# Attention and feed-forward on one core: the first batch's q and k in token halves from two queues, and a planner that models the DMA queues as rings

## The chip, the cores and the metric

The kernel runs on one core of a Trainium2 chip. The metric is device time in microseconds (us) of one execution, as the median of several runs. A profile shows one execution; its span runs from the first to the last instruction of the core. TensorE (PE) multiplies matrices, ScalarE (ACT) does activations and issues some DMAs, VectorE (DVE) and GpSimd (POOL) do elementwise work, SyncE (SP) only issues DMAs.

## The reference

There are 8 batches of 8 heads, 576 tokens, head size 64. Attention has a forget gate per token; its output, tokens by 512, goes through a gated feed-forward network (512 to 1536 and back).

```python
scores = scale * np.matmul(q, k.transpose(0, 1, 3, 2))
cum = np.cumsum(np.log(np.clip(f, 0.0001, 1.0)), axis=-1)
scores = np.where(causal, -1e9, scores + cum[..., :, None] - cum[..., None, :])
attn = softmax(scores)                       # max-shifted, over the last axis
x = (attn @ v)                               # (B, H, S, D) -> (B*S, H*D)
xn = x / np.sqrt(np.mean(x * x, -1, keepdims=True) + 1e-6) * rms_g
g = xn @ w_gate
out = (g * sigmoid(g) * (xn @ w_val)) @ w_out
```

## The kernel before

The work is written as some thousands of pieces (`plan.add`): name, engine, an assumed duration, what it depends on, which buffers it takes and gives back, a priority. `Plan.run` is a list scheduler at build time: it plays the pieces through with their assumed durations, and the order in which they start there is the order in which the instructions are emitted. On the chip each engine then works its own list strictly in that order, and waits for real. So a plan's durations never run on the chip; only its order does.

On PE the pieces are of kind A (attention: transposes, scores, values) or F (feed-forward: gates and projections). `LEAD` and `UNTIL` steer the mix: A comes first as long as less of A is done than a line that reaches all of A when the share `UNTIL` of F is done.

```python
behind = a_done < self.lead + (a_total - self.lead) * min(1.0, f_done / (f_total * self.until))
first = "A" if behind else "F"
```

A batch b goes through these steps. q and k come from memory into `st` tiles and are cast to bf16 `ld` tiles. For b = 0 and 1 (`PE_TURN`) PE transposes them (L462) and ACT and DVE keep the results in `QK` (L467); for the others SP issues DMA transposes (L493, the last 64 tokens L496). Scores (L561) go to PSUM, ACT exponentiates (L569), POOL masks the diagonal blocks (L577), PE multiplies with the scaled V (values, L596), DVE normalizes into `x` (L606). Then ACT squares the five token blocks (L613), POOL makes the root (L622), DVE scales to `xn` (L626), and `xn` is transposed into `xT`, by PE for b = 0 and 1 (L651), else by DMA (L645). Batch 0 is split: part one (`HEAD`) does tokens 0 to 255, part two (`REST`) the others.

The feed-forward goes by groups of tokens: g0 and g1 have 256, g2 to g9 have 512. A group has 12 steps of gate and value matmuls (L747, four each), ACT tanh `th` (L752), DVE `ga` and `hT` (L756, L762); then the projections (L768, 12 matmuls for 128 tokens), ACT's copy to `ores` (L773) and the store, which ACT issues (L776). Group g(n) from g2 on needs the `xT` of batch n-1, g1 that of batch 0.

q and k of batch 0 come as four units, each of two heads (`load_runs`: 128 partitions, 512 tokens, 256 KB), k and q in turn, all issued by SP. DVE casts k, POOL casts q. The weights are loaded by POOL in eight pieces of columns; in the plan all of them wait for q's last cast.

The framework gives every DMA that SP or ACT issues one of eight semaphores in turn, in the order in which they are emitted. Before it issues, the engine waits until the DMA that had this semaphore before, eight places ahead, has landed. In the built program's order this wait reads `DMAHW0_49` to `DMAHW7_49`. The planner has a pool of eight for it (`hw`), of which it takes whichever is free.

The planner before keeps one clock for all DMAs: each transfer begins when the last one has ended.

Of the kernel before, what the change touches and what calls it, by code (L numbers as in the profile page):

```python
# [11 lines left out]
ACT = mybir.ActivationFunctionType  # L12
# [9 lines left out]
LEAD, UNTIL = 30.0, 0.74  # L22
Q_AHEAD, V_AHEAD, T_AHEAD = 1.6, 0.9, 0.95
SPLIT, PE_TURN = (0,), (0, 1)
GROUPS = ((0, 256), (256, 512)) + tuple((a, a + 512) for a in range(512, B * S, 512))
N_ST, N_LD, N_PT, N_XN = 10, 6, 4, 5
SV_PRIO = -0.7
# [25 lines left out]
class Plan:  # L53
# [7 lines left out]
    TO = {"PE": 0.20, "ACT": 0.07, "DVE": 0.07, "POOL": 0.08, "SP": 0.05}  # L61

# [11 lines left out]
    def run(self):  # L74
# [17 lines left out]
        dma_free, t, order = 0.0, 0.0, []  # L92
        n_left, next_seq = len(self.pieces), 0

# [15 lines left out]

        while n_left:
            moved = False
            for e in self.ENGINES:
# [5 lines left out]
                if e == "PE":  # L119
                    behind = a_done < self.lead + (a_total - self.lead) * min(1.0, f_done / (f_total * self.until))  # L120
                    first = "A" if behind else "F"
                    p = min(c, key=lambda p: (p.kind != first, p.prio))
                    if p.kind == "A":
                        a_done += p.dur
                    else:
                        f_done += p.dur
                else:
                    p = min(c, key=lambda p: p.prio)
                ready[e].remove(p)
# [4 lines left out]
                if p.xfer is None:  # L134
                    p.done = p.end
                else:
                    dma_free = max(dma_free, p.start + 0.7) + p.xfer
                    if e == "SP":
                        p.end = free_at[e] = max(p.end, dma_free - 2.0)
                    p.done = max(dma_free, p.end) + 1.7  # L140
                for pool, key in p.acq:
                    if key not in held:
# [4 lines left out]
                        slots[i] = float("inf")  # L147
                for key in p.rel:
                    left[key] -= 1
                    freed[key] = max(freed.get(key, 0.0), p.done + 0.08)  # L150
                    if not left[key]:
                        pool, i = held[key]
                        self.pools[pool][i] = freed[key]
                for u in p.users:
                    lat = 0.0 if u.eng == e and p.xfer is None else self.TO[e]
                    u.ready = max(u.ready, p.done + (0.02 if p.xfer is not None else lat))
                    u.nwait -= 1
                    if not u.nwait:
                        ready[u.eng].append(u)
# [5 lines left out]
            nxt = [f for f in free_at.values() if f > t + 1e-9]  # L165
            nxt += [p.ready for e in self.ENGINES for p in ready[e] if p.ready > t + 1e-9]
            nxt += [f for s in self.pools.values() for f in s if t + 1e-9 < f < float("inf")]
            assert nxt, "the plan is stuck at " + str([p.name for e in self.ENGINES for p in ready[e]])
            t = min(nxt)
        return sorted(order, key=lambda p: p.start)  # L170
# [28 lines left out]
def kernel(  # L199
# [65 lines left out]
    lf = plan.add("lf", "SP", 0.6, load_f, xfer=0.4, prio=(-9,), acq=[("hw", "lf"), ("pt", "pre")], rel=["lf"])  # L265
# [57 lines left out]

    def load_rg():
# [3 lines left out]
    p_rg = plan.add("rg", "SP", 0.6, load_rg, xfer=0.7, prio=(-8,), acq=[("hw", "rg")], rel=["rg"])  # L328
# [8 lines left out]
    for i, (c0, c1) in enumerate(WCH):  # L337
        for n, w, src in (("wg", wg, moe_w_gate), ("wv", wv, moe_w_val)):
            nm = f"{n}{i}"
            p = plan.add(nm, "POOL", 0.75, lambda w=w, src=src, c0=c0, c1=c1: load_w(w, src, c0, c1),  # L340
                         xfer=(22 + 37 * (c1 - c0) / 256) * 512 / 16e3, prio=(W_PRIO[i],), acq=[("sw", nm)], rel=[nm])
# [8 lines left out]
    p_wo = [plan.add(f"wo{i}", "POOL", 0.75, lambda i=i: load_wo(i), xfer=4.6, prio=(WO_PRIO[i],),  # L350
# [10 lines left out]
    def attention(b):  # L361
# [30 lines left out]
        def cast(src, dst, eng, runs=False):  # L392
# [5 lines left out]
            (nc.vector if eng == "DVE" else nc.gpsimd).tensor_copy(o, x)  # L398
# [17 lines left out]
        for u in range(4):  # L416
            for nm, src in (("k", k), ("q", q)):
                key = f"{nm}{b}.{u}"
                if not pe and nm == "k":
                    ld[nm, u] = plan.add("L" + key, "POOL", 0.9, lambda nm=nm, src=src, u=u: load_cast(nm, src, u), xfer=2.1,  # L420
                                         acq=[("ld", key), ("sw", "h" + key)], rel=["h" + key], prio=(ahead + 0.01 * u,), seq=True)
                    continue
                fn = load_runs if pe else load_rows
                a = plan.add("L" + key, "SP", 0.6, lambda fn=fn, nm=nm, src=src, u=u: fn(nm, src, u), xfer=0.78 if pe else 1.2,
                             acq=[("st", "s" + key), ("hw", "h" + key)], rel=["h" + key], prio=(ahead + 0.01 * u,), seq=True)
                eng = "DVE" if b == 0 and nm == "k" else "POOL"
                ld[nm, u] = plan.add("C" + key, eng, 0.55 if eng == "DVE" else 0.62,
                                     lambda nm=nm, u=u, eng=eng: cast((nm + "s", b, u), (nm, b, u), eng, pe), [a],
                                     acq=[("ld", key)], rel=["s" + key], prio=(ahead + 0.01 * u,))
        key = f"qk{b}"  # L430
        a = [plan.add(f"L{key}{t}", "SP", 0.45, lambda t=t, src=src: load_tail(t, src), xfer=0.6,
# [406 lines left out]
```

## Time and profile before

| | us |
|---|---|
| runs | 430.77, 428.05, 429.48; median 429.48 |
| profiled execution | 429.98 |
| its span | 428.2 |
| outside the span | 1.8 |
| PE busy in the span | 375.9 (88%) |

A row in order of time reads: start, duration, engine, line, operation, output and input tile, count; in brackets the idle time of the engine just before, and what ended it. SPq and ACTq are the queues on which SP and ACT issue DMAs. PEclk is the granted TensorE clock, 1.00 being 2.4 GHz and 0.50 being 1.2 GHz.

### The profile page before, as it was taken

Reading aid. Unit: us, or ns where it says so; the run is one execution under the profiler, and the core shown is the slowest. Engines: PE = TensorE matmul, PEld = TensorE weight load, DVE = VectorE, ACT = ScalarE, POOL = GpSimd, SP = SyncE. Lnnn points to the kernel's source line nnn. Section 1 sums busy time; section 2 is a strip of 40 time slices with the busy share of each in tenths; the row PEclk is TensorE's granted clock in tenths of the full one; section 3 lists DMA queues with packets and bytes.
Section 4 is the critical chain, followed back from the end, with each engine's and each line's share of the span. In section 5 each row is a group of like instructions: output and inputs, shape, how many; then the busy total and the mean of one; then the engine's idle time right before and its main releaser. Section 6 shows DMA issues by size and latency. Waiting matters only on the chain.

```text
span 428.2 us, 8052 instructions
## 1 busy us (share of the span) xinstructions
PE 375.9 (88%) x3085; PEld 195.0 (46%) x3085; DVE 239.6 (56%) x462; ACT 218.7 (51%) x361; POOL 163.2 (38%) x259
## 2 busy tenths in 40 slices
PE   1559889969998799799997999499989996999996
PEld 1327657634643355335543554145534552444442
DVE  5654846745763577347623686057546743770760
ACT  2664477557751574447655763157646752332321
POOL 3791457437530483119332843047315411000000
PEclk9999999979999899989996999889999998999999
DMA  7999995769927997369967983799457004001002
GB/s 232 194 282 196 205 185 57 100 147 167 88 51 143 215 102 91 105 145 174 101 124 147 181 87 81 135 221 74 77 148 143 2 26 119 10 2 73 24 2 99
DMA packets 155847, 50.89 MB, mean 119 GB/s; under 512 B 141280, under 2 KB 151008, under 8 KB 155808
## 3 DMA queue, kind: packets, MB, share of 16 engines
q1 hardware_dynamic: 119872, 33.06, 43.3%
q0 software_dynamic: 30752, 7.87, 18.7%
q10 hardware_dynamic: 5184, 9.44, 6.2%
q8 instruction: 24, 0.39, 0.4%
q14 instruction: 15, 0.12, 0.1%
HBM read 38.16 MB, written 9.44 MB: 111 GB/s over the span
## 4 chain that ended last, share of the span: by engine, by line
PE 61%; DVE 11%; DMA 7%; ACT 7%; issue 5%; POOL 5%; SPq 3%; ACTq 1%; POOLq 0%; DVEq 0%
PE ff L747 41%; PE ff L768 10%; PE sc L561 5%; DVE xn L626 3%; DMA xT<-xn 3%; DVE x L606 3%; ACT junk L613 3%; PE po L596 2%; DVE ga L756 2%; DMA QK<-ld 2%; SPq L645 2%; PE ff L596 2%; POOL PT L577 2%; DVE hT L762 1%; ACT th L752 1%
## 5 line engine op out<-in xcount | busy, mean ns | idle before, releaser
L747 PE MATMUL ff<-xT,wg 128*128 128x512 bf16 (+1 forms) x480 | 120.2, 375 | 11.5 <-DMA xT<-xn 4.5
L756 DVE SCALAR_TENSOR_TENSOR ga<-th,ff 128x512 f32<-128x512 f32 (+1 forms) x120 | 76.0, 633 | 95.5 <-ACT th L752 95.4
L747 PE MATMUL ff<-xT,wv 128*128 128x512 bf16 (+1 forms) x480 | 118.0, 370 | 6.5 <-DVE ga L756 5.7
L752 ACT ACTIVATE th<-ff 128x512 f32<-128x512 f32 (+1 forms) x120 | 66.3, 555 | 92.5 <-PE ff L747 76.0
L569 ACT ACTIVATE PT<-sc 128x1024 bf16<-128x1024 f32 (+2 forms) x100 | 95.8, 988 | 29.9 <-PE sc L561 27.8
L768 PE MATMUL ff<-wo,hT 128*128 128x512 bf16 x432 | 95.4, 379 | 0.1
L762 DVE SCALAR_TENSOR_TENSOR hT<-ga,ff 128x512 bf16<-128x512 f32 (+1 forms) x120 | 76.1, 634 | 17.9 <-PE ff L747 7.3
L747 PEld LDWEIGHTS <-wg 128*128 128x128 bf16 x480 | 45.9, 101 | 62.4 <-issue 21.3
L747 PEld LDWEIGHTS <-wv 128*128 128x128 bf16 x480 | 46.3, 101 | 57.4 <-issue 17.4
L768 PEld LDWEIGHTS <-hT 128*128 128x128 bf16 x432 | 41.9, 98 | 50.0 <-issue 0.6
L577 POOL TENSOR_SCALAR_AFFINE_SELECT PT<-PT 128x1024 bf16<-128x1024 bf16 (+1 forms) x44 | 38.4, 884 | 41.9 <-ACT PT L569 41.2
L626 DVE SCALAR_TENSOR_TENSOR xn<-x,rs,rgb 128x512 bf16<-128x512 f32 x40 | 30.6, 818 | 37.6 <-POOL rs L622 37.6
L773 ACT COPY ores<-ff 128x512 f32<-128x512 f32 x36 | 20.9, 581 | 51.6 <-PE ff L768 29.1
L561 PE MATMUL sc<-QK 64*128 64x128 bf16 (+2 forms) x328 | 31.2, 291 | 6.4 <-DMA QK<-ld 2.5
L596 PEld LDWEIGHTS <-PT 128*128 128x128 bf16 x896 | 32.6, 99 | 6.3 <-POOL PT L577 0.9
L405 POOL TENSOR_TENSOR Vs<-st,decT 128x512 bf16<-128x512 f32 x28 | 29.2, 1044 | 11.9 <-DMA st<-in_v_dram 11.8
L398 POOL CAST ld<-st 128x512 bf16<-128x512 f32 x44 | 27.8, 653 | 12.8 <-DMA st<-in_q_dram 7.8
L613 ACT ACTIVATE junk<-x 128x512 bf16<-128x512 f32 x40 | 25.2, 630 | 13.5 <-DVE x L606 10.7
L561 PEld LDWEIGHTS <-QK 64*128 64x128 bf16 x584 | 17.5, 98 | 25.4 <-issue 20.0
L521 POOL COPY K<-QT 64x256 bf16<-64x256 bf16 x16 | 7.5, 471 | 55.7 <-DMA QT<-ld 53.3
L619 POOL TENSOR_SCALAR ms<-sq 128x5 f32<-128x5 f32 (+2 forms) x9 | 1.8, 198 | 56.0 <-ACT junk L613 56.0
L377 POOL DMA_DIRECT2D ld<-in_k_dram x24 | 21.9, 916 | 0.0
(66 smaller groups left out, 224.7 us busy)
## 6 DMA issues: line engine op xcount, KB each, us to landing
out_dram<-ores ACTq DMA_DIRECT2D x36, 256.0 KB, 2.1
st<-in_q_dram SPq DMA_DIRECT2D x32, 256.0 KB, 5.2
st<-in_v_dram SPq DMA_DIRECT2D x32, 256.0 KB, 4.8
ld<-in_k_dram POOLq DMA_DIRECT2D x24, 128.0 KB, 4.2
st<-in_k_dram SPq DMA_DIRECT2D x8, 256.0 KB, 6.7
wo<-in_moe_w_out_dram POOLq DMA_DIRECT2D x2, 768.0 KB, 24.4
st<-in_q_dram SPq DMA_DIRECT2D x8, 128.0 KB, 4.9
st<-in_k_dram SPq DMA_DIRECT2D x8, 128.0 KB, 4.3
```

The costliest lines, as they stand in the source:

```text
L405: e.tensor_tensor(Vs[i][:, j, :, 0:D], t, bcast(dj, D), ALU.mult)
L561: nc.tensor.matmul(sc[:, par, c:c + n], lhsT=k_cols(r, p, kj), rhs=q_cols(r, p, q0, n), start=True, stop=True)
L569: nc.scalar.activation(T["pt", b, p][:, :, c0:c0 + n], T.pop(("sc", b, p, c0))[:, :, 0:n], ACT.Exp, scale=scale)
L577: nc.gpsimd.affine_select(out=d, in_=d, pattern=[[0, m], [1, 128]], compare_op=ALU.is_ge, fill=0.0, base=0, channel_multiplier=-1)
L596: nc.tensor.matmul(T["po", b, hs][:, qm, m, :], lhsT=w, rhs=Vs[i][:, kj, h, :], start=(kj == 0), stop=(kj == qi))
L613: nc.scalar.activation(junkp.tile([128, DM], BF16, name="junk"), T["x", b][:, j, :], ACT.Square, accum_out=T["sq", b, js][:, j:j + 1])
L626: nc.vector.scalar_tensor_tensor(xn, in0=T["x", b][:, j, :], scalar=T["rs", b, js][:, j:j + 1], in1=rgb, op0=ALU.mult, op1=ALU.mult)
L747: nc.tensor.matmul(ps[:, 0:w], lhsT=wt[:, dc, fc * 128:(fc + 1) * 128], rhs=T["xT", g][:, dc, 0:w], start=(dc == 0), stop=(dc == NDC - 1))
L752: nc.scalar.activation(t[:, 0:w], T["pg", g, fc][:, 0:w], ACT.Tanh, scale=0.5)
L756: nc.vector.scalar_tensor_tensor(a[:, 0:w], in0=T.pop(("th", g, fc))[:, 0:w], scalar=1.0, in1=T.pop(("pg", g, fc))[:, 0:w], op0=ALU.add, o ...
L762: nc.vector.scalar_tensor_tensor(T["hT", g][:, fc, 0:w], in0=T.pop(("ga", g, fc))[:, 0:w], scalar=0.5, in1=T.pop(("pv", g, fc))[:, 0:w], o ...
L768: nc.tensor.matmul(po, lhsT=T["hT", g][:, fc, j * 128:(j + 1) * 128], rhs=wo[:, fc, :], start=(fc == 0), stop=(fc == NFC - 1))
```

## The change

1. Batch 0's q and k come as other units: a unit u now holds tokens 0 to 255 (u = 0, 1) or 256 to 511 (u = 2, 3) of four heads, and is loaded by two DMAs of 64 partitions each (two heads each). q's are issued by ACT, k's by SP. `keep` writes the transposed unit to two head pairs at once. q's casts of u = 0, 1 move from POOL to ACT.
2. The order of loads in batch 0: units 0 and 1, two tiles of V, units 2 and 3, the tails, the rest of V.
3. `rms_g` is issued by ACT, not by SP.
4. In the plan each weight piece depends on another piece (`W_AFTER`): the first two on q's second cast, the others on loads of V of batch 0 and 1.
5. The planner has a ring for each issuing queue. The rings share the DMA in proportion to a weight of their first transfer, and an issue that overfills its ring of 128 holds its engine. Transfers are now (time alone, weight, descriptors in a ring).
6. `UNTIL` goes from 0.74 to 0.70. As the planner's model is another, the order of all engines is another, to the end of the program.

```diff
-LEAD, UNTIL = 30.0, 0.74
+LEAD, UNTIL = 30.0, 0.7
...
+W_AFTER = ("Cq0.1", "Cq0.1", "Lv0.2", "Lv0.2", "Lv0.40", "Lv0.40", "Lv0.40", "Lv0.40", "Lv1.3", "Lv1.3")
...
+    RING, LAND = 128, 1.75
...
+        def shares():
+            busy = [e for e in ring if ring[e]]
+            total = sum(ring[e][0][0].xfer[1] for e in busy)
+            return {e: ring[e][0][0].xfer[1] / total for e in busy}
...
+                    if c[1].eng in ("SP", "ACT") and waiting(c[1].eng) > self.RING:
+                        full[c[1].eng] = c[1]
+                        free_at[c[1].eng] = never
...
-                    dma_free = max(dma_free, p.start + 0.7) + p.xfer
-                    if e == "SP":
-                        p.end = free_at[e] = max(p.end, dma_free - 2.0)
-                    p.done = max(dma_free, p.end) + 1.7
...
-        nc.sync.dma_start(out=rgb, in_=bass.AP(tensor=moe_rms_g.tensor, offset=moe_rms_g.offset,
+        nc.scalar.dma_start(out=rgb, in_=bass.AP(tensor=moe_rms_g.tensor, offset=moe_rms_g.offset,
...
-        if b == 0:
-            for x in first_w:
-                x.deps += [ld["q", 3]]
...
+        def load_half(nm, src, u, e):
+            hh, z = divmod(u, 2)
+            t = stage((nm + "s", b, u))[e * 64:e * 64 + 64, :].rearrange("p (h c) -> p h c", h=2)
+            pp = 2 * z + e
+            (nc.scalar if nm == "q" else nc.sync).dma_start(
+                out=t, in_=src[b, 2 * pp:2 * pp + 2, hh * 256:hh * 256 + 256, :].rearrange("h (p i) d -> p h (i d)", i=4))
...
+                        eng = "DVE" if nm == "k" else "ACT" if u < 2 else "POOL"
...
+        if split:
+            load_qk((0, 1))
+            load_v((0, 1))
+            load_qk((2, 3))
+            load_tails()
+            load_v((2, 3, 4))
...
+                if split:
+                    hh, z = divmod(pp, 2)
+                    src = src.rearrange("p (i e m) -> p e m i", i=4, e=2)
+                    dst = QK[i][:, 2 * z:2 * z + 2, t, hh * 256:hh * 256 + 256].rearrange("p e (m i) -> p e m i", i=4)
...
+    for p, after in zip(first_w, W_AFTER):
+        p.deps.append(of_name[after])
```

Three places of the built programs show what moved.

**The start, ACT.** `PT_134` and `PT_136` are the forget gates (log, then exp), `rgb` is `rms_g`, `st` the loaded q. Before:

```order
L271 ACT_TABLE_LOAD
L271 ACTIVATE PT_134<-PT_134 64x576 [waits DVE_49]
L467 COPY QK0_112<-ff_172 128x512 [waits PE_49]
L285 ACT_TABLE_LOAD [waits DVE_49]
L285 ACTIVATE PT_134<-PT_134,mid_167 64x576 [waits Activation_49]
```

Now:

```order
L386 DMA rgb_107<-in_moe_rms_g_dram 128x512 [waits DMAHW0_49]
L330 ACT_TABLE_LOAD
L330 ACTIVATE PT_136<-PT_136 64x576 [waits DVE_49]
L481 DMA st_167<-in_q_dram 64x2x256 [waits DMAHW6_49]
L459 CAST ld_177<-st_124 128x512 [waits DMAHW2_49]
L459 CAST ld_180<-st_147 128x512 [waits DMAHW4_49]
L564 COPY QK0_112<-ff_182 128x2x256 [waits PE_49]
L344 ACT_TABLE_LOAD [waits DVE_49]
L344 ACTIVATE PT_136<-PT_136,mid_172 64x576 [waits Activation_49]
```

Loads and casts of q now stand in ACT's list among the gate's steps; four issues of q stand ahead of the first row shown, and three more (for u = 2 and 3) come between the exponentials of part one.

**The start, POOL.** `wg` and `wv` are the gate and value weights. Before:

```order
L398 CAST ld_162<-st_146 128x512 [waits DMAHW3_49,Pool_49]
L398 CAST ld_184<-st_151 128x512 [waits DMAHW5_49]
L398 CAST ld_203<-st_156 128x512 [waits DMAHW7_49]
L398 CAST ld_223<-st_170 128x512 [waits DMAHW1_49,DVE_49,PE_49]
L334 DMA wg_109<-in_moe_w_gate_dram 128x4x256
```

Now:

```order
L369 COPY tri_105<-tri2_142 64x64 [waits Pool_49]
L370 COPY tri_105<-tri2_142 64x64
L395 DMA wg_109<-in_moe_w_gate_dram 128x4x256
L395 DMA wv_110<-in_moe_w_val_dram 128x4x256
L680 AFFINE_SELECT PT_225<-PT_225 128x2x128 [waits Activation_49,Pool_49]
```

The casts that stood ahead of the first weight load, and waited for q, are gone from there; the first two weight loads have no wait.

**The start of group g4, DVE.** `xn` of batch 3 feeds it; `hT_2777` and, in the changed program, `hT_3064` are its output tiles, `x_2388` and `x_2275` the x of batch 3, `x_2840` that of batch 4. Before:

```order
L606 TENSOR_TENSOR x_2388<-ff_2614,rden_2645 128x5x64
L626 SCALAR_TENSOR_TENSOR xn_2719<-x_2388,rs_2698,rgb_107 128x512
L626 SCALAR_TENSOR_TENSOR xn_2722<-x_2388,rs_2698,rgb_107 128x512
L626 SCALAR_TENSOR_TENSOR xn_2740<-x_2388,rs_2698,rgb_107 128x512
L626 SCALAR_TENSOR_TENSOR xn_2743<-x_2388,rs_2698,rgb_107 128x512
L626 SCALAR_TENSOR_TENSOR xn_2746<-x_2388,rs_2698,rgb_107 128x512
L756 SCALAR_TENSOR_TENSOR ga_2774<-th_2767,ff_2756 128x512
L762 SCALAR_TENSOR_TENSOR hT_2777<-ga_2774,ff_2762 128x512
```

Now:

```order
L729 SCALAR_TENSOR_TENSOR xn_2772<-x_2275,rs_2690,rgb_107 128x512
L729 SCALAR_TENSOR_TENSOR xn_2775<-x_2275,rs_2690,rgb_107 128x512
L729 SCALAR_TENSOR_TENSOR xn_2779<-x_2275,rs_2690,rgb_107 128x512
L708 RECIPROCAL rden_2841<-po_2803 128x5
L709 TENSOR_TENSOR x_2840<-po_2803,rden_2841 128x5x64
L708 RECIPROCAL rden_2857<-ff_2823 128x5
L709 TENSOR_TENSOR x_2840<-ff_2823,rden_2857 128x5x64
L708 RECIPROCAL rden_2937<-po_2903 128x5
L709 TENSOR_TENSOR x_2840<-po_2903,rden_2937 128x5x64
```

The group's first `ga` no longer stands directly behind the last `xn`: six of the eight heads of the next batch come between, and `ga_3061` with `hT_3064` only behind them.

**The stores of g3, ACT.** Before:

```order
L773 COPY ores_2713<-ff_2672 128x512 [waits DMAHW3_49,PE_49]
L776 DMA out_0_dram<-ores_2713 128x512 [waits DMAHW7_49,Activation_49]
L773 COPY ores_2737<-ff_2700 128x512 [waits PE_49]
L776 DMA out_0_dram<-ores_2737 128x512 [waits DMAHW3_49,Activation_49]
L773 COPY ores_2748<-ff_2724 128x512 [waits DMAHW6_49,PE_49]
L776 DMA out_0_dram<-ores_2748 128x512 [waits DMAHW2_49,Activation_49]
L752 ACTIVATE th_2767<-ff_2756 128x512 [waits PE_49]
```

Now:

```order
L879 COPY ores_2799<-ff_2757 128x512 [waits DMAHW1_49,PE_49]
L882 DMA out_0_dram<-ores_2799 128x512 [waits DMAHW7_49,Activation_49]
L672 ACTIVATE PT_2770<-sc_2781 128x2x512 [waits PE_49]
L672 ACTIVATE PT_2770<-sc_2786 128x2x512 [waits PE_49]
L879 COPY ores_2879<-ff_2844 128x512 [waits DMAHW4_49,PE_49]
L882 DMA out_0_dram<-ores_2879 128x512 [waits DMAHW3_49,Activation_49]
L672 ACTIVATE PT_2898<-sc_2869 128x2x512 [waits PE_49,Pool_49]
L672 ACTIVATE PT_2898<-sc_2874 128x2x512 [waits PE_49]
```

The four stores of a group stood together between two groups; now exponentials of the next batch stand between them.

## Rows read from the trace of the kernel before

**Rows 1.** The page's busy time of each engine, and the answer on span and clock.

```profile
PE 375.9 (88%) x3085; PEld 195.0 (46%) x3085; DVE 239.6 (56%) x462; ACT 218.7 (51%) x361; POOL 163.2 (38%) x259
core 0: 428.2 us, clock 0.964
```

**Rows 2.** Busy time by stretch: stretch, its length, each engine; clock, DMA share, GB/s.

```profile
0.00:33.90 33.90, 14.39 (x141) 9.58 (x142) 18.76 (x46) 17.93 (x26) 23.05 (x45) 1.00 1.10 234
91.50:428.20 336.70, 310.59 (x2348) 149.62 (x2348) 186.32 (x325) 167.66 (x269) 112.95 (x171) 0.96 0.61 103
...
100.00:120.00 20.00, 20.00 (x235) 11.16 (x234) 14.71 (x30) 14.26 (x18) 14.72 (x22) 1.00 1.00 109
```

**Rows 3.** What PE waited for from 60 us on: total us, times, longest.

```profile
PE ff L747 <- DVE ga L756: 5.9, 3, 4.4
PE ff L747 <- DMA xT<-xn: 4.5, 2, 3.8
PE ff L651 <- DVE xn L626: 3.8, 2, 3.3
PE ff L747 <- issue: 3.3, 1, 3.3
PE sc L561 <- DMA QK<-ld: 2.5, 1, 2.5
PE ff L747 <- ACT ores L773: 2.4, 2, 1.4
```

**Rows 4.** The start in order of time, to the first gate matmul.

```profile
0.79 1.28 ACT L271 ACT_TABLE_LOAD   x1 [0.79 <-PEq L822]
4.18 0.68 ACT L271 ACTIVATE PT<-PT 64x576 f32<-64x576 f32 x1 [2.10 <-DVE PT L268]
10.28 0.59 ACT L467 COPY QK<-ff 128x512 bf16<-128x512 bf16 x1 [5.41 <-PE ff L462]
12.18 0.78 ACT L285 ACTIVATE PT<-PT,mid 64x576 f32<-64x576 f32 x1
13.80 0.81 ACT L569 ACTIVATE PT<-sc 128x768 bf16<-128x768 f32 x1
16.92 2.28 ACT L569 ACTIVATE PT<-sc 128x768 bf16<-128x768 f32 x3
30.17 1.71 DVE L626 SCALAR_TENSOR_TENSOR xn<-x,rs,rgb 128x512 bf16<-128x512 f32 x2 [4.20 <-POOL rs L622]
33.91 1.01 PE L747 MATMUL ff<-xT,wg 128*128 128x256 bf16 x4 [0.67 <-ACT xT L660]
```

**Rows 5.** DMA issues of the first 60 us, and of 10 to 30 us: KB, us to landing.

```profile
PT<-in_f_dram SPq DMA_DIRECT2D x1, 144.0 KB, 2.9
...
st<-in_q_dram SPq DMA_DIRECT2D x4, 256.0 KB, 7.7
```

**Rows 6.** PE from the last values of batch 3 to group g4.

```profile
167.83 0.19 PE L596 MATMUL ff<-Vs,P 128*128 128x65 bf16 x1
...
182.81 1.87 PE L747 MATMUL ff<-xT,wg 128*128 128x512 bf16 x4 [3.33 <-issue]
184.47 1.80 PE L747 MATMUL ff<-xT,wv 128*128 128x512 bf16 x4
186.11 1.03 PE L747 MATMUL ff<-xT,wg 128*128 128x512 bf16 x4
186.97 1.03 PE L747 MATMUL ff<-xT,wv 128*128 128x512 bf16 x4
```

**Rows 7.** ACT's last copy and store of g2.

```profile
135.34 0.59 ACT L773 COPY ores<-ff 128x512 f32<-128x512 f32 x1 [2.26 <-PE ff L768]
...
140.26 0.41 ACTq L776 DMA_DIRECT2D out_dram<-ores  x1
```

**Rows 8.** PE from the last values of batch 7 to group g8.

```profile
349.02 0.19 PE L596 MATMUL ff<-Vs,P 128*128 128x65 bf16 x1
...
360.76 1.86 PE L747 MATMUL ff<-xT,wg 128*128 128x512 bf16 x4 [3.78 <-DMA xT<-xn]
```

More of the change, by code (lines that the diff above doesn't have):

```diff
@@ L91, in run @@
         a_done = f_done = 0.0
-        dma_free, t, order = 0.0, 0.0, []
+        t, order = 0.0, []
         n_left, next_seq = len(self.pieces), 0
+        ring = {e: [] for e in self.ENGINES}
+        coming, full = [], {}
+        never = float("inf")
         def free(pool, t):
@@ L109, in can, with finish @@
             return all(free(pool, t) >= n for pool, n in need.items())
+        def finish(p):
+            for key in p.rel:
+                left[key] -= 1
+                freed[key] = max(freed.get(key, 0.0), p.done + 0.08)
+                if not left[key]:
+                    pool, i = held[key]
+                    self.pools[pool][i] = freed[key]
+            for u in p.users:
+                lat = 0.0 if u.eng == p.eng and p.xfer is None else self.TO[p.eng]
+                u.ready = max(u.ready, p.done + (0.02 if p.xfer is not None else lat))
+                u.nwait -= 1
+                if not u.nwait:
+                    ready[u.eng].append(u)
@@ new lines, in dma_to @@
+        def dma_to(t):
+            while dma_t[0] < t - 1e-9:
+                step = min(t, max(dma_next(), dma_t[0] + 1e-7))
+                sh = shares()
+                for e, s in sh.items():
+                    ring[e][0][1] -= s * (step - dma_t[0])
+                dma_t[0] = step
+                for e in sh:
+                    if ring[e][0][1] <= 1e-6:
+                        p = ring[e].pop(0)[0]
+                        p.done = step + self.LAND
+                        finish(p)
+                for c in [c for c in coming if c[0] <= step + 1e-9]:
+                    coming.remove(c)
+                    ring[c[1].eng].append([c[1], c[1].xfer[0]])
+                    if c[1].eng in ("SP", "ACT") and waiting(c[1].eng) > self.RING:
+                        full[c[1].eng] = c[1]
+                        free_at[c[1].eng] = never
+                for e in list(full):
+                    if waiting(e) <= self.RING + 1e-6:
+                        full.pop(e).end = free_at[e] = step
@@ L146, in run @@
                         held[key] = (pool, i)
[L147 to L159, printed above, removed]
+                        slots[i] = never
+                if p.xfer is None:
+                    p.done = p.end
+                    finish(p)
+                else:
+                    coming.append((p.end, p))
                 order.append(p)
@@ L397, in cast @@
                 x = x.rearrange("p (h i d) -> p i h d", i=4, h=2)
-            (nc.vector if eng == "DVE" else nc.gpsimd).tensor_copy(o, x)
+            {"DVE": nc.vector.tensor_copy, "POOL": nc.gpsimd.tensor_copy, "ACT": nc.scalar.copy}[eng](o, x)
         def scale_v(j, eng):
@@ L415, in attention @@
         ahead = b - Q_AHEAD if not pe else b - 3
[L416 to L429, printed above, removed]
```

149 lines of the change are left out of this document (106 added, 43 removed).

## The prediction

> **What bounds the kernel now.** I read the busy times first, then the stretches, then PE's waits, then PE in order of time where the waits are long. PE is the busiest engine, at 375.9 of 428.2 us, and no other passes 56% [rows 1]. Its work is the same in both programs: the same matmuls stand in both orders. So the time can only come from PE's idle time and from time at the half clock. Two places hold it. Up to the first gate matmul PE is busy 14.4 of 33.9 us, and from 91.5 us on 310.6 of 336.7 [rows 2]. Between groups lies nearly all of the latter: where attention and feed-forward are mixed, as from 100 to 120 us, PE is busy 20.00 of 20 us at full clock [rows 2]. The long waits after 60 us are 5.9 + 4.5 + 3.8 + 3.3 + 2.5 + 2.4 = 22.4 us [rows 3], and they stand at the starts of g2 to g8.
>
> The start of g4 shows the mechanism. Batch 3's last values end at 168.02, and the first gate comes at 182.81: 14.8 us for x, squares, root, xn and the transposes by DMA. PE has only four gate matmuls and the 48 projections of g3 to do meanwhile, 52 x 0.2165 = 11.3 us, and waits 3.33 [rows 6]. (0.2165 is a quarter of the step of 0.86 from one gate to the next at full clock.) The clock then costs more: the first two gates follow at steps of 1.66 and 1.64, so PE was at 1.2 GHz after the wait and lost 2 x 0.8 = 1.6 us. Seven such places make 11.2 us, which fits into the 0.036 x 428.2 = 15.4 us that the mean clock of 0.964 makes of the span [rows 1].
>
> A second mechanism is ACT's queue. g2's last store was ready at 135.93 and issued at 140.26 [rows 7]: its semaphore belonged to a DMA transpose that SP issued late, and ACT, which works in order, held tanh and exponentials back for 4.3 us.
>
> **The change part by part.**
>
> *The order after the start.* This is the large term. I counted PE's rows in the two built orders, with 0.2165 us for a matmul of 512 columns, 0.031 for one of values and some 0.55 for a visit of scores. Between a batch's last values and the first gate that needs it stands, for g2 to g8: before 6.9, 14.8, 11.3, 9.0, 17.4, 10.4, 7.8 us of PE work; now 16.4, 17.4, 26.0, 21.1, 40.8, 22.2, 13.0. For g4 these are 92 matmuls of gates and projections (19.9), 90 of values (2.8) and six visits of scores (3.3). The chain needs 14.8 us where two and a half blocks must be transposed [rows 6] and 11.5 where a group needs but the first block, as g8 does (349.21 to 360.76) [rows 8]. So g4 to g7 have cover to spare, g3 has 2.6 us, g8 1.5. In the mix, ACT's squares share their engine with tanh and exponentials, which makes the chain longer. For g2 PE itself transposes, and 7.2 us of work stand ahead of that where before 5.4 and a wait of 3.3 did; so I leave 1.8 us of waiting at g2 and 1.5 at g8.
>
> The stores now stand between exponentials. What is queued behind a held store are exponentials, tanh and copies, and PE waits for those. I compared each store with the DMA eight places ahead of it, in us of PE work between the two. Before, eight stores had less than 6 us (2.8 to 5.5), and g2's last, at 5.5, is the one that was held 4.3. Now three have: 3.6, 5.1 and 5.6. A hold costs PE between nothing (other work is queued) and 4.3 each, 0 to 13 us; I take 5.
>
> Idle time: 22.4 goes, 1.8 + 1.5 + 5 = 8.3 comes. Clock: 11.2 goes, three places at 1.6 stay, 5. Net 22.4 + 11.2 - 8.3 - 5 = 20.3 us.
>
> *The start.* Part one needs half of q and k, not all. But the steps on ACT get longer. rgb's issue waits for q's first half; the loads of the first microseconds land after 2.9 us at best and 7.7 in the crowd [rows 5]. From an issue at 0.8 that is 3.7 to 8.5; with two queues at work I take 4.5. The issue and the table load of 1.28, which before lay at 0.79 under f's load, put the log at 6.3 and its end at 7.0; before it began at 4.18 [rows 4]. Then an issue (0.5), two casts of 0.59 (a copy's price), transposes (0.4 more), a copy of 0.59, the second table load 1.28, the exponential 0.78, the second copy, four exponentials of part one at 0.81 and two issues between them: 7.0 + 0.9 + 1.2 + 0.4 + 0.6 + 1.3 + 0.8 + 0.6 + 3.2 + 0.9 = 16.9. Before the last of them ended at 19.2 [rows 4]. DVE and POOL work beside this and are idle or ahead.
>
> The last half of q is issued by ACT only behind these exponentials, at 17.4. It lands 2.9 to 7.7 later; I take 4.5, as the first weights are gone by then: 21.9. Cast, transposes, copy, square and root, five steps of at most 0.85 (one of the two xn of 1.71), give 26.1 for xn. From xn to the first gate it was 33.91 - 30.17 = 3.7, so the gate comes at 29.9, between 28.3 and 33.1. The lead is 4.0, between 0.8 and 5.6. PE has done 0.7 us less of work by then (four banks of scores are still to come, a transpose is done early), which makes 3.3; I take 3. The K4 copies, the tails' casts and three weight issues on POOL stand ahead of the root, and I hide them under the wait for q's last half; uncovered they would cost 2.3 us of issues.
>
> *Weights.* That they are gated is true of the plan alone. In POOL's order the first two stand without a wait behind the mask's copies, which end at some 2.5 us, so they run beside the first halves of q and k. They write 0.5 MB; at the 234 GB/s of the start [rows 2] that is 2.2 us of all engines, of which the first loads lose a part: 0 to 2.2, and the 4.5 above holds 0.8 of it. The last weights go out later than before; they are needed by the fifth step of g0 and later, and the projections' weights not before g0's own projections.
>
> *Halves and two queues.* The trace has no half tile. My sum takes nothing from the second queue as such: the gain at the start comes from the tokens that part one no longer waits for, and the bounds of the landing, 2.9 and 7.7 us, hold for halves too. The Trainium skill speaks against this part: its page DMA: Bandwidth & Descriptors, section Rules for kernel authors, says that two transfers to disjoint partition halves serialize on the same 16 engines, and that one transfer of 128 partitions should be used; nothing here shows it yet. By that rule alone the start would give nothing, 3 us less than my sum.
>
> The sum: 429.98 (span 428.2 and 1.8 around it) - 20.3 - 3 = 406.7 for a profiled execution. That one stands 0.5 above the median of the runs, so I forecast **406**.
>
> **The rivals.**
>
> *A, held stores take half.* All three near stores hold ACT for 4.3 us in the middle of exponentials, 13 in place of 5, and each wait brings its stretch at half clock (3 us more): 417. For it: ACT has one list, and the exponentials stand right behind the stores. Against: before, eight such stores stood near, and two long waits came of them (the 4.4 in the first of [rows 3], and most of the 2.4).
>
> *B, only the start counts.* The planner's order holds only as long as its durations do; if batches run late, the gates wait as before, at other places. Then 429.5 - 3 = 426.5, or 429.5 if the start gives nothing either. Against it: the mixed stretches run on the chip without a gap [rows 2].
>
> *C, slower.* If SP runs behind its plan by 2 us, stores up to 7.5 us from their DMA are held too; these are eight more, eleven in all, between exponentials. At 3.8 us each, the wait at g8 being the size [rows 8], that is 42 in place of 5: 443. The time of before is reached at the eighth held store (23.3 / 3.8, and the 5 already counted); below that the filled group starts still pay. For it: SP's transposes wait for xn and for casts, and so pass any lateness on. Against: the stores' distances were laid out with a model of DMA that is closer than the one before, in which near stores were three times as many.
>
> *D, the halves bring nothing* (the two queues serialize, or the ungated weights push the first loads back by all of 2.2 us and q's last half lands at 25): the start gives nothing or loses 1, and the rest stays: 410. This is inside the forecast's range.
>
> **How the numbers follow.** Forecast with D: 0.66, its own range 398 to 414. A 0.17, B 0.09, C 0.08. The range of 8 in 10 takes in the forecast's cases and A with some 5 us around it: 394 to 423. Below 394 everything that I leave of waits (13.3 us) would have to be gone. About 1%, 4.3 us, is what a measurement of this kernel can tell from no change. Faster by more than that: the forecast, A, and a small part of B: 0.84. Within 1%: most of B, 0.07. Slower: C and a remainder, 0.09.
>
> **What would show it.** In the profile after, the stretch to the first gate should end near 30 us. PE's waits for xT, xn and ga at the starts of g3 to g7 should be gone, and the mean clock should be above 0.98. The last store of a group should be issued within 1 us of its copy in most groups. The first two weight loads should be issued near 2.5 us. I am wrong if PE's waits add up to 20 us again after 60 us, whoever they wait for; if those are exponentials behind stores, A or C is the cause, if they are xT, B.

## The result, and the profile after

| | before | after |
|---|---|---|
| median of the runs, us | 430.08 (4 runs) | 415.40 (411.34 to 419.30, 4 runs) |
| profiled execution, us | 429.98 | 414.88 |
| span, us | 428.2 | 413.2 |
| PE's waits after 60 us, all rows | 25.8 | 18.7 |

The ratio is 0.9635, with a 95% interval of 0.9553 to 0.9717; the run of 419.30, in a slower state that some executions show, is left out of it. The profiled execution gained 15.1 us where 23.3 were forecast. Below, "PE's waits" is the sum of all rows of the view of [rows 3], and a store is "held" from the end of its copy to its issue.

The page's busy times and the answer on span and clock, of the changed kernel:

```profile
PE 365.2 (88%) x3042; PEld 191.9 (46%) x3085; DVE 245.0 (59%) x462; ACT 217.0 (53%) x363; POOL 170.1 (41%) x257
core 0: 413.2 us, clock 0.991
```

Of PE's records 43 are missing here (3042 against the 3085 of [rows 1]), so its busy time reads low; waits and clock are what can be compared. The clock went from 0.964 to 0.991: (1 - clock) x span fell from 15.4 to 3.7 us. That and the 7.1 us less of waits make 18.8, more than the gain of 15.0 of the span, since the clock is low during waits too, and such time is counted twice. One such stretch of the kernel before (times; busy us of PE, PEld, DVE, ACT, POOL; then the clock), the end of the wait of 4.4 of [rows 3]:

```profile
274.77:278.00 3.23, 0.00 (x1) 0.00 (x1) 0.69 (x1) 1.08 (x2) 0.54 (x2) 0.50 0.79 111
```

The start gave 0.5. What PE waited for from 60 us on:

```profile
PE ff L853 <- DVE ga L862: 9.5, 8, 4.1
PE ff L754 <- DVE xn L729: 3.6, 2, 3.2
PE ff L754 <- DVE ga L862: 1.6, 3, 0.9
PE po L699 <- POOL PT L680: 1.3, 2, 1.1
```

No gate waits for xT any more, as two did in [rows 3] and a third, at g4, under "issue". But a wait for `ga` of 4.1 stands there, and one for `xn` of 3.2. The start in order of time (PE, ACT, DVE, POOL put together), to the first gate (the row of x is the last of part one, `junk` is the square of a token block):

```profile
6.14 0.68 ACT L330 ACTIVATE PT<-PT 64x576 f32<-64x576 f32 x1
9.64 0.61 ACTq L481 DMA_DIRECT2D st<-in_q_dram  x1
10.29 1.14 ACT L459 CAST ld<-st 128x512 bf16<-128x512 f32 x2 [3.48 <-DMA st<-in_q_dram]
18.23 0.60 ACTq L481 DMA_DIRECT2D st<-in_q_dram  x1
18.82 0.80 ACT L672 ACTIVATE PT<-sc 128x768 bf16<-128x768 f32 x1
21.62 0.42 DVE L709 TENSOR_TENSOR x<-ff,rden 128x256 f32<-128x256 f32 x1
23.71 0.63 ACT L716 ACTIVATE junk<-x 128x512 bf16<-128x512 f32 x1
24.03 1.18 POOL L459 CAST ld<-st 128x512 bf16<-128x512 f32 x2 [1.93 <-DMA st<-in_k_dram]
26.50 0.59 ACT L564 COPY QK<-ff 128x512 bf16<-128x512 bf16 x1 [2.07 <-DVE QK L564]
26.99 0.63 ACT L716 ACTIVATE junk<-x 128x512 bf16<-128x512 f32 x1
29.14 1.65 DVE L729 SCALAR_TENSOR_TENSOR xn<-x,rs,rgb 128x512 bf16<-128x512 f32 x2
33.43 0.85 PE L853 MATMUL ff<-xT,wg 128*128 128x256 bf16 x3
```

Against [rows 4] the log begins 2 us later (6.14 for 4.18), the last exponential of part one ends at 19.6 in place of 19.2, and the first gate comes 0.48 earlier. The first two weight loads were issued at 2.44 and 3.44, as forecast. The longest wait that is left, in order of time on ACT, then on PE:

```profile
138.50 0.59 ACT L879 COPY ores<-ff 128x512 f32<-128x512 f32 x1 [0.41 <-ACT ores L879]
143.79 0.34 ACTq L882 DMA_DIRECT2D out_dram<-ores  x1
144.18 1.02 ACT L672 ACTIVATE PT<-sc 128x1024 bf16<-128x1024 f32 x1 [5.09 <-DMA QK<-ld]
145.10 0.59 ACT L858 ACTIVATE th<-ff 128x512 f32<-128x512 f32 x1
...
146.46 1.86 PE L853 MATMUL ff<-xT,wv 128*128 128x512 bf16 x4 [4.14 <-DVE ga L862]
```

The copy ends at 139.09 and its store is issued at 143.79: held for 4.70 us, as the store of [rows 7] was. Exponential and tanh stand behind it, PE waits 4.14, and the four matmuls behind that take 1.86, where four take 1.03 at full clock [rows 6]: the half clock. Four stores are held over 1 us (2.65, 4.70, 3.05 and 4.15), a fifth 0.93; each goes out 0.1 us after the landing of the DMA of SP that had its semaphore before. The last stores of eight of the ten groups go out within 0.03 us of their copies. The kernel before, measured in the same way, held nine stores, 21.8 us in all.

### The profile page after: what moved, and what is told of

It is laid out like the page before. It is cut to its first block, busy times and chain, and to the rows that moved or that the text cites. A ratio compares the mean times of both kernels' runs of the same rounds, so it can differ in the third digit from the quotient of the medians.

```text
span 413.2 us, 8034 instructions
## 1 busy us (share of the span) xinstructions
PE 365.2 (88%) x3042; PEld 191.9 (46%) x3085; DVE 245.0 (59%) x462; ACT 217.0 (53%) x363; POOL 170.1 (41%) x257
## 4 chain that ended last, share of the span: by engine, by line
PE 50%; DVE 17%; ACT 9%; DMA 8%; POOL 5%; issue 5%; SPq 3%; ACTq 1%; DVEq 0%; POOLq 0%
PE ff L853 26%; PE ff L874 14%; DVE xn L729 5%; DVE ga L862 5%; ACT junk L716 4%; DVE hT L868 4%; PE sc L664 3%; PE po L699 3%; DMA st<-in_q_dram 3%; DMA QK<-ld 2%; PE ff L699 2%; ACT th L858 2%; SPq L596 2%; ACT PT L672 2%; POOL PT L680 1%
## 5 line engine op out<-in xcount | busy, mean ns | idle before, releaser
L853 PE MATMUL ff<-xT,wv 128*128 128x512 bf16 (+1 forms) x464 | 113.6, 362 | 11.8 <-DVE ga L862 9.9
L853 PE MATMUL ff<-xT,wg 128*128 128x512 bf16 (+1 forms) x467 | 113.5, 362 | 2.5 <-ACT ores L879 1.1
L874 PEld LDWEIGHTS <-hT 128*128 128x128 bf16 x432 | 41.0, 98 | 48.4 <-issue 1.5
L879 ACT COPY ores<-ff 128x512 f32<-128x512 f32 x36 | 21.1, 585 | 60.8 <-PE ff L874 41.0
L729 DVE SCALAR_TENSOR_TENSOR xn<-x,rs,rgb 128x512 bf16<-128x512 f32 x40 | 40.0, 1020 | 1.5 <-POOL rs L725 1.5
L699 PEld LDWEIGHTS <-PT 128*128 128x128 bf16 x896 | 32.5, 98 | 10.9 <-POOL PT L680 5.2
L466 POOL TENSOR_TENSOR Vs<-st,decT 128x512 bf16<-128x512 f32 x28 | 30.6, 1093 | 5.6 <-DMA st<-in_v_dram 5.5
L708 DVE RECIPROCAL rden<-po 128x5 f32<-128x5 f32 (+2 forms) x31 | 5.9, 191 | 39.8 <-PE po L699 39.3
L459 POOL CAST ld<-st 128x512 bf16<-128x512 f32 x42 | 26.2, 644 | 3.2 <-DMA st<-in_k_dram 1.9
L438 POOL DMA_DIRECT2D ld<-in_k_dram x24 | 21.9, 919 | 0.0
L699 PE MATMUL ff<-Vs,PT 128*128 128x65 bf16 x476 | 20.8, 196 | 0.8 <-POOL PT L680 0.8
```

The source lines that it names most:

```text
L466: e.tensor_tensor(Vs[i][:, j, :, 0:D], t, bcast(dj, D), ALU.mult)
L699: nc.tensor.matmul(T["po", b, hs][:, qm, m, :], lhsT=w, rhs=Vs[i][:, kj, h, :], start=(kj == 0), stop=(kj == qi))
L729: nc.vector.scalar_tensor_tensor(xn, in0=T["x", b][:, j, :], scalar=T["rs", b, js][:, j:j + 1], in1=rgb, op0=ALU.mult, op1=ALU.mult)
L853: nc.tensor.matmul(ps[:, 0:w], lhsT=wt[:, dc, fc * 128:(fc + 1) * 128], rhs=T["xT", g][:, dc, 0:w], start=(dc == 0), stop=(dc == NDC - 1))
L874: nc.tensor.matmul(po, lhsT=T["hT", g][:, fc, j * 128:(j + 1) * 128], rhs=wo[:, fc, :], start=(fc == 0), stop=(fc == NFC - 1))
```

## The experiments

Two theories stood against each other after the result. **O**: the changed planner's order covers the starts of the groups, and that is the gain. **S**: the new loads make it. What both rest on was counted in the built orders as in the prediction, the cover: us of PE work between a batch's last values and the first gate that needs it. The runs were timed on several chips, each beside the kernel before; so the ratios are what can be compared, and two ratios with overlapping intervals are not told apart.

| kernel | cover g2 to g8 | us | ratio to before, 95% interval | first gate | PE's waits after 60 us |
|---|---|---|---|---|---|
| before | 6.9 14.8 11.3 9.0 17.4 10.4 7.8 | 430.08 | 1 | 33.91 | 25.8 |
| changed | 16.4 17.4 26.0 21.1 40.8 22.2 13.0 | 415.40 | 0.9635 (0.9553 to 0.9717) | 33.43 | 18.7 |
| planner, old loads | 7.5 20.4 15.7 25.2 29.8 22.7 13.0 | 419.54 | 0.9739 (0.9685 to 0.9794) | 30.61 | 20.5 |
| new loads, old planner | 16.4 13.0 22.3 29.5 18.2 24.4 13.0 | 417.02 | 0.9701 (0.9649 to 0.9754) | 41.95 | 14.6 |
| the same, weights in a lump | 6.9 14.8 11.3 9.0 17.4 10.4 7.8 | 429.73 | 1.0016 (0.9987 to 1.0044) | 34.48 | 25.2 |
| changed, UNTIL 0.74 | 16.4 17.4 26.0 21.1 21.7 11.6 13.0 | 420.37 | 0.9739 (0.9663 to 0.9815) | 33.10 | 19.7 |
| planner, old loads, weights spread | 14.8 17.9 26.9 20.6 27.2 22.7 13.0 | 408.29 | 0.9540 (0.9480 to 0.9599) | 29.09 | 16.4 |
| that, and two q tiles by POOL | 14.2 14.5 14.7 18.6 22.8 22.7 13.0 | 406.05 | 0.9474 (0.9421 to 0.9528) | 29.67 | 13.3 |

**1. The planner alone.** Batch 0 is loaded as before:

```diff
-                    if split:
+                    if False:
                         a = [plan.add(f"L{key}{e}", "ACT" if nm == "q" else "SP", 0.42,
...
-        p.deps.append(of_name[after])
+        p.deps.append(of_name["Cq0.3"])
```

> The changed planner with batch 0's q, k and rms_g loaded as before (whole units of two heads, all issued by SP, weights behind q's last cast). Theory O (the gain is the order that the planner sets after the start; the start gives 0.5 us, 33.43 against 33.91): PE's waits after 60 us stay under 20 us, clock above 0.98, time 413 to 419. Rival S (the new loads shift everything that follows, and the order pays only with them): time above 424, PE's waits after 60 us 22 us or more.

Measured: 419.54, between the two: theory O's waits and clock were missed as well (20.5 us, 0.958). The first gate came at 30.61, nearly 3 us ahead of the changed kernel's. Six stores were held, 21.5 us in all, against four and 14.6 (without the one of 0.93).

**2. The new loads alone.** The planner's `run` and UNTIL of before, everything else as changed.

> The new loads of batch 0 (halves, two issuing queues, weights in the plan behind other pieces) with the planner and UNTIL of before. Theory O: the long waits at the starts of the groups are there again, 20 us or more after 60 us, clock near 0.965, time 426 to 432. Rival S: time below 420.

Measured: 417.02, the time of Rival S, though the first gate comes 8 us later than before (41.95). Theory O failed here: the old planner made an order with a cover as good as the new one's. Its waits show no xT either:

```profile
PE ff L800 <- DVE ga L809: 4.3, 3, 2.9
PE sc L611 <- ACT PT L619: 4.1, 3, 3.4
PE ff L701 <- DVE ga L809: 3.3, 4, 2.0
```

**3. Weights in a lump.** Of run 2 this takes one thing back, what each weight piece waits for in the plan:

```diff
-        p.deps.append(of_name[after])
+        p.deps.append(of_name["Cq0.3"])
```

> As the run with the new loads and the planner of before (417.0), but with all ten weight pieces behind q's last cast in the plan, as before. Between a batch's last values and the first gate of g2 to g8 stand then 6.9, 14.8, 11.3, 9.0, 17.4, 10.4, 7.8 us of PE work, as in the kernel before; with the weights spread it was 16.4, 13.0, 22.3, 29.5, 18.2, 24.4, 13.0. Theory C (this cover sets the time, whichever part of the change makes it): the long waits at g2 to g8 are back, 20 us or more of PE's waits after 60 us, time 425 to 431. Rival N (the new loads themselves save the time): 420 or less.

Measured: 429.73, the time of before, and its waits one by one as in [rows 3]:

```profile
PE ff L800 <- DVE ga L809: 5.8, 3, 4.4
PE ff L800 <- DMA xT<-xn: 4.2, 2, 3.7
PE ff L701 <- DVE xn L676: 3.8, 2, 3.3
PE ff L800 <- issue: 3.4, 1, 3.4
PE sc L611 <- DMA QK<-ld: 2.7, 1, 2.7
```

So one line, `W_AFTER`, is worth 12.7 us under the old planner, with loads that by themselves give nothing. The old planner counts all DMAs on one clock, and its ten weight pieces are 4 x 1.89 + 4 x 3.07 + 2 x 4.6 = 29.0 us of that clock by the code's own numbers; in a lump they stand ahead of the next batches' loads. That this is why the attention falls behind in that plan is argued from the code; that spreading them moves the cover and the time is shown.

**4. UNTIL back at 0.74**, in the changed kernel.

> The changed kernel with UNTIL back at 0.74. Theory O with the planner's model of DMA as its cause: time within 412 to 420. Rival U (UNTIL makes the order that covers the group starts, the model of DMA nothing): the waits at g4 to g8 come back, time 424 to 430.

Measured: 420.37 (415.00 to 424.66), at the edge of the first, and not told apart from the changed kernel. No gate waits for xT, so the waits of Rival U did not come back. Cover changed at g6 and g7 alone; eight stores were held, 22.0 us in all. In the kernel before, UNTIL at 0.70 gives word for word the order of 0.74, so it does nothing by itself.

**5. Weights really gated.** A copy of one column stands ahead of the first weight load on POOL:

```diff
-        nc.gpsimd.dma_start(out=w[:, :, c0:c1], in_=src[:, c0:c1].rearrange("(c p) f -> p c f", p=128))
+        w is wg and c0 == 0 and nc.gpsimd.tensor_copy(consts.tile([128, 1], BF16, name="seen"), st["q", 0, 1][:, 0, 0, 0:1]); nc.gpsimd.dma_start(out=w[:, :, c0:c1], in_=src[:, c0:c1].rearrange("(c p) f -> p c f", p=128))
...
```

> The changed kernel with one POOL copy of one column of q's second cast tile ahead of the first weight load, so that the weights really wait for it; the order of all else is the same. Theory W (the ungated weights hold the first q and k back, which is why the start gave 0.5 us where 4 were forecast): q's first casts start near 8 in place of 10.29, the last k of part one is cast near 9 in place of 11.67, first gate 31 to 32, time 1.5 to 2.5 us under the changed kernel's. Rival H (halves and queues themselves are slow, the weights have no part): casts of q at 10 or later, first gate at 33 to 34.5, time the same within 1 us or later by up to 1.

Measured: 413.30, ratio 0.9598 (0.9546 to 0.9649). That is 2.1 us under the changed kernel, as theory W had it, but the intervals overlap, and the first gate is Rival H's. ACT's casts of q moved only from 10.29 to 9.41, k's second cast from 11.67 to 9.38, and nothing of it reached the gate:

```profile
9.41 1.14 ACT L459 CAST ld<-st 128x512 bf16<-128x512 f32 x2 [2.53 <-DMA st<-in_q_dram]
...
24.34 1.16 POOL L459 CAST ld<-st 128x512 bf16<-128x512 f32 x2 [2.14 <-DMA st<-in_v_dram]
...
33.71 0.63 PE L853 MATMUL ff<-xT,wg 128*128 128x256 bf16 x2
```

POOL's casts at 24.3, of q's and the tails' last parts, stand where they stood. The ungated weights cost part one 0.9 to 2.3 us and the first gate nothing.

**6. All halves from SP.**

```diff
-            (nc.scalar if nm == "q" else nc.sync).dma_start(
+            nc.sync.dma_start(
```

> The changed kernel with the halves of q issued by SP, at the same places of the order; all queues' orders are else the same. Theory B (the bytes set the start; the second queue brings nothing): first gate within 1 us of 33.43, time within 1.5 us of the changed kernel's; ACT's log then begins near 4.2 as before, and the loss is SP's issues, some 0.7 us each. Rival Q (two queues feed the start, one can't): q's second cast at 12.5 or later in place of 10.9, first gate at 35 or later, time 2 us or more above.

Measured: 417.20, ratio 0.9722 (0.9662 to 0.9782), not told apart from the changed kernel. The second cast of q came at 12.66 in place of some 10.9, as Rival Q had it, but POOL's casts at 24.52 and the gate at 33.90, as theory B had it: the second queue brings part one 1.8 us and the first gate 0.5.

**7. Four held stores by POOL.**

```diff
-            nc.scalar.dma_start(out=out[t0 + j * 128:t0 + (j + 1) * 128, :], in_=T.pop(("o", g, j)))
+            (nc.gpsimd if (g, j) in ((2, 1), (2, 3), (3, 3), (4, 0)) else nc.scalar).dma_start(out=out[t0 + j * 128:t0 + (j + 1) * 128, :], in_=T.pop(("o", g, j)))
```

> The changed kernel with four stores (the second and fourth of g2, the fourth of g3, the first of g4: those that ACT held for 2.65, 4.70, 3.05 and 4.15 us) issued by POOL, on its software queue; the order of PE, DVE and SP is the same. Theory H (held stores make the long waits inside the mix): PE's waits of 4.14 at 146.46 and 2.19 at 194.33 are gone, and the half clock behind the first of them; time 5 to 8 us under the changed kernel's, 407 to 411. Rival L (ACT's exponentials are late for another reason, for example the transposes by DMA that the scores need): the two waits stay, time within 1 us of the changed kernel's.

Measured: 415.99, ratio 0.9691 (0.9635 to 0.9747). Both waits are gone, as theory H said, and the time is the same, as Rival L said. PE's order is that of the changed kernel, so the starts of ACT's copies (L879) can be laid side by side: this run is 2.8 us late at the changed kernel's 132.03, 0.2 late at 175.29, and 4.3 late at 180.63. The 2.6 us won are lost at the next wait, one of 3.96 for a mask at 179.95.

**8. Three scalings of V on DVE.** An `xn` of batch 0's second part (the expectation takes it for one of batch 1) took 4.22 us, and PE waited 3.23 for it at 62.40:

```profile
L729 DVE SCALAR_TENSOR_TENSOR xn<-x,rs,rgb x40: 739/766/4221, 29.1 to 340.2; 128x512 bf16<-128x512 f32 x40
```

(min, median and maximum in ns.)

```diff
-            e = nc.vector if eng == "DVE" else nc.gpsimd
+            e = nc.vector if eng == "DVE" or (b, j) in ((1, 1), (1, 2), (1, 3)) else nc.gpsimd
```

> The changed kernel with three of batch 1's scalings of V (tiles 1 to 3) on DVE in place of POOL; PE's order is the same. In the changed kernel an xn of batch 1 took 4.22 us where 0.77 is usual, beside five POOL instructions in a row, and PE waited 3.23 for it at 62.40. Theory P (POOL's work in a row kept DVE's instruction out): all xn take 0.74 to 1.2 us, the wait at 62.40 falls below 1.3, time 2 to 4 us under the changed kernel's. Rival D (the xn waited for something else): one xn still takes over 3 us, time the same or, as DVE has 2.8 us more work there, up to 2 us above.

Measured: 415.03, ratio 0.9644 (0.9577 to 0.9712). Theory P holds: the longest `xn` is 1.54 us and the wait 1.21. Again the time is the same. The copies are level with the changed kernel's at 132.03, 2.8 us early at 175.29, and 2.6 late at 180.63. In this run, POOL and then PE:

```profile
165.12 1.04 POOL L466 TENSOR_TENSOR Vs<-st,decT 128x512 bf16<-128x512 f32 x1 [2.51 <-DMA st<-in_v_dram]
...
175.81 1.09 POOL L680 TENSOR_SCALAR_AFFINE_SELECT PT<-PT 128x1024 bf16<-128x1024 bf16 x1
...
176.96 0.95 PE L699 MATMUL po<-Vs,PT 128*128 128x65 bf16 x14 [3.98 <-POOL PT L680]
```

POOL waits for a load of V, works off the scalings of V, a root and a smaller mask without a gap, and only then makes this one. That mask ends at 176.9 in the changed kernel too, where POOL was late behind squares of ACT, and PE came late and waited but 1.11. What a wait at 146 gives back ends at this mask, here behind a load that SP issues.

**9. A planner that knows the semaphores' turn.**

```diff
-            return all(free(pool, t) >= n for pool, n in need.items())
+            if "hw" in need and len(turn) >= 8 and turn[-8].done > t + 1e-9:
+                return False
+            return all(free(pool, t) >= n for pool, n in need.items() if pool != "hw")
```

> The changed kernel with a planner that knows the semaphores' turn: a DMA of SP or ACT starts in the plan only when the one eight places ahead of it has landed, in place of a pool of eight of which any free one is taken. Theory H: stores are planned where they need not wait; all holds over 0.9 us add up to under 6 us where it was 15.5, time 408 to 413. Rival T (SP runs later on the chip than in any plan, so the holds stay whatever the plan knows): holds of 10 us or more, time 413 to 419.

Measured: 413.47, ratio 0.9642 (0.9572 to 0.9711). Five stores are held, 15.5 us: Rival T, by its time and its holds. The plan starts no store that must wait, and on the chip each of the five waits for a transpose or a load that SP issued.

**10. The planner, the old loads, and the weights spread.** Run 1 with `W_AFTER`, the first two behind q's last cast.

> As the run with the changed planner and the old loads (419.5; first gate 30.61; 7.5 us of PE work ahead of g2's first gate), with the weights spread over the start of the program as the change has them, the first two behind q's last cast. The cover of g2 to g8 is then 14.8, 17.9, 26.9, 20.6, 27.2, 22.7, 13.0 us of PE work. Theory C (cover sets the time, and the old loads are no worse at the start): first gate 30 to 32, clock 0.98 or more, time 408 to 414. Rival L (late stores and late loads of SP, 21.5 us of holds in that run, set the time whatever the cover): time 416 to 421.

Measured: 408.29, theory C's time, 11.3 us under run 1. Its reason holds only in part. The one cover that was short in run 1 is that of g2 (7.5, now 14.8), and PE's waits there were 2.1 us. The rest of the gain lies in waits inside the mix, which no cover counts, and in the half clock behind them: from the first gate on, (1 - clock) x time fell from 14.1 to 5.0 us. (The mean clock of 0.971 misses theory C's 0.98 by a stretch at half clock from 15 to 32 us, most of it ahead of the gate.) Five stores are held, 15.9 us in place of 21.5. The start:

```profile
12.35 0.62 POOL L459 CAST ld<-st 128x512 bf16<-128x512 f32 x1 [1.52 <-DMA st<-in_q_dram]
...
22.03 0.42 DVE L709 TENSOR_TENSOR x<-ff,rden 128x256 f32<-128x256 f32 x1
22.63 0.63 ACT L716 ACTIVATE junk<-x 128x512 bf16<-128x512 f32 x1
23.39 0.63 ACT L716 ACTIVATE junk<-x 128x512 bf16<-128x512 f32 x1
...
25.68 1.90 DVE L729 SCALAR_TENSOR_TENSOR xn<-x,rs,rgb 128x512 bf16<-128x512 f32 x2 [0.81 <-POOL rs L725]
...
29.09 1.01 PE L853 MATMUL ff<-xT,wg 128*128 128x256 bf16 x4 [0.67 <-ACT xT L763]
```

q's last cast stands at 12.35, where in the changed kernel it stood at 24.03. Part one's x is ready no earlier than there (22.45 for 22.04), but both squares follow it at once.

**11. Two q tiles of four by POOL**, in the changed kernel, from batch 2 on.

```diff
-                    elif not pe and nm == "k":
+                    elif not pe and (nm == "k" or u < 2):
```

> The changed kernel with two of the four q tiles of batches 2 to 7 loaded by POOL with the cast in the load (as k's are), so that SP issues 12 loads less and POOL casts 12 tiles less. Cover of g2 to g8: 15.9, 14.6, 26.9, 23.2, 25.2, 22.2, 13.0. Theory S (SP's lateness against the plan holds the stores and the loads of V): holds of stores fall from 14.6 to under 8 us, PE's waits after 60 us from 18.7 to under 14, time 408 to 413. Rival G (what SP saves, POOL's longer list costs, its masks being the next thing late): PE waits more for masks, time 414 to 419.

Measured: 410.57, ratio 0.9560 (0.9513 to 0.9608), 4.8 us under the changed kernel, though the intervals overlap. The time is theory S's, its cause is not: the holds are 15.5 us, as the changed kernel's are with the one of 0.93. PE's waits are 15.0 and the slow `xn` (run 8) is gone with the order. Why it gained, if it did, is not settled.

**12. Runs 10 and 11 together.**

> The best so far (changed planner, old loads, weights spread: 408.3) with two of the four q tiles of batches 2 to 7 loaded by POOL with the cast in the load, which alone took the changed kernel to 410.6. Cover of g2 to g8: 14.2, 14.5, 14.7, 18.6, 22.8, 22.7, 13.0. Theory A (the two gains are at different places and add): first gate 29 to 30, time 402 to 406. Rival O (both only move the same waits, which the order sets anew in each program): time 407 to 412, with waits of 2 us and more on masks or xT at other places than before.

Measured: 406.05 (405.50 to 408.72, 6 runs), the lowest median, and between the two ranges. It is 2.2 us under run 10 where theory A had some 4.8, but the intervals of the two overlap, so whether anything adds is not shown. Three stores are held, 5.7 us, and waits of 3.4 and 2.6 stand at new places, as theory O had it:

```profile
PE ff L853 <- DVE ga L862: 4.2, 9, 1.0
PE sc L632 <- POOL K L624: 3.4, 1, 3.4
PE po L699 <- POOL PT L680: 2.6, 1, 2.6
```

## Why the prediction was right, and where it was not

**The order after the start** (forecast 20.3, measured some 14.5: the span's 15.0 less 0.5 of the start). The mechanism was right as to what sets the time: run 3 against run 2 changes nothing but the order, with planner and loads held fixed, and the time moves by 12.7 us. That cover is what counts in an order is read from the waits: run 3 waits for xT at the group starts as the kernel before does, run 2 nowhere. Gates that waited for xT had 7.8 to 11.3 us of cover in the kernel before, and with 13 or more in the changed one none did; the limit is not sharp, as one with 14.6 waited 3.0 in run 11. Cover is not all, as run 10 against run 1 shows.

What was mis-sized is the idle time. The forecast had 22.4 - 8.3 = 14.1 us less of it; the rows have 25.8 - 18.7 = 7.1. Of what was allowed for, 1.3 came at g2 (1.8 forecast), none at g8 (1.5) and 6.3 behind held stores (5). With no term in the sum came 4.1 at g1, most of it the one `xn`, and 7.0 in waits of 1.4 and less, against which the kernel before had 3.4 beside the long waits. The clock was nearly right: beside the waits 14.5 - 7.1 = 7.4 us are left for it, and 6.2 were forecast. Two waits with half clock behind them are left, not three.

**Held stores.** In the kernel before, all eight stores that stood nearest to their DMA were held, 1.3 to 4.3 us, and not g2's last alone; so the change did not add holds, it took some away. In the changed kernel, of the three nearest two were held (2.65 and 4.15), and two others, 4.70 and 3.05: there distance in PE work is a poor guide, because SP is late by its own measure. Runs 7 and 8 show that such a wait costs less than its length: part of it was cover for the next thing that is late.

**The rivals.** Rival A's time, 417, lies nearer to the median of 415.4 than the forecast's 406, but not for A's reason: waits behind stores were 6.3 us, not 13. B and C did not happen: no gate waits for xT, and all holds together are 15.5 us, where C had 42 of them.

**The start** (forecast -3, measured -0.5). This step failed. Part one did come forward: its x is ready at 22.04, and was ready at 24.44 in the kernel before, whose row this is:

```profile
24.02 0.42 DVE L606 TENSOR_TENSOR x<-ff,rden 128x256 f32<-128x256 f32 x1
```

From there to the first gate the changed kernel takes 11.4 us, before 9.5, in run 10 but 6.6. In ACT's list the two squares of part one (23.71 and 26.99 in the rows above) each stand behind a copy of the other tokens' q or k, the second behind the copy at 26.50 that waits for q's last half. In run 10, where whole units bring x no later (22.45), both squares stand right behind it. The sum did lead the gate through q's last half, and each step there took longer: that half was cast at 24.03 (forecast landing 21.9), from there to xn it took 5.1 us (4.2), and from xn to the gate 4.3 (3.7), as PE waited for a transpose placed ahead of the gate. That moving the squares would give the lead back is argued from these rows; no run moved them alone.

Rival D had the gain at the start right, and nearly the time of q's last half (25), but neither of its causes is the main one: run 5 takes the ungated weights away and run 6 the second queue, and the gate stays. With the changed planner whole units from one queue bring the gate to 30.61 and 29.09; with the old one they gave 33.91. So the planner by itself brings the gate forward, and the new loads, as its order has them, take that back. What is left as the cause on their side is that V and the second halves come in another order, and the halves themselves. Bytes moved in the first 25 us, changed kernel, then run 10:

```profile
DMA packets 10070, 5.18 MB, mean 207 GB/s; under 512 B 6113, under 2 KB 9878, under 8 KB 10070
```

```profile
DMA packets 10922, 6.07 MB, mean 243 GB/s; under 512 B 6043, under 2 KB 10729, under 8 KB 10921
```

The ten kernels with halves moved 191 to 210 GB/s there, the four with whole units 228 to 248. The Trainium skill (DMA: Bandwidth & Descriptors, Rules for kernel authors) says that two transfers to halves by partition serialize, and that one transfer of 128 partitions is to be used. These rates are in keeping with that, and do not prove it: halves and the order of V were not tried apart, so how much each costs stays open.

**Weights.** I priced part 4 of the change only as traffic at the start, 0 to 2.2 us. There it cost the first casts 0.9 to 2.3 us and the gate nothing. Its effect is on the order: 12.7 us (run 3) and 11.3 us (run 10). That a dependence in the plan moves all later work was not among my terms.

## What to carry to other kernels

Where a planner sets the order, change one input at a time and count the cover in the built order first: here one tuple of weight dependences carried most of a gain that a new DMA model seemed to bring. Price a wait by what is late next, not by its length: two repairs that each removed waits of 2 to 6 us left the time as it was, because a late mask took its place. Loads that let part of the work begin early pay only if no in-order list puts the other part's steps ahead of the early part's, as ACT's list did with the squares.

## What was not expected of the hardware

An `xn` on DVE (two inputs in SBUF) took 4.22 us in place of 0.77 while POOL ran five instructions without a gap, from 58.55 to 62.4 (run 8); with three of POOL's scalings gone the longest was 1.54. The Trainium skill (SBUF — State Buffer, Who interferes with whom) says that DVE and GpSimd share a port pair under an exclusive lock. The trace agrees, with those 4.22 us. But DVE waited through several of POOL's instructions in turn, where the section on the two sides of SBUF on the same page speaks of one whole instruction.
